# Window attention with a gated feed-forward: all local scores on the two row halves of the tensor engine, in bursts of four banks

## The chip, the cores and the metric

The kernel runs on one core of one Trainium2 chip. The metric is the device time of one execution in microseconds (us); the median of several is quoted. The engines are PE (TensorE), DVE (VectorE), ACT (ScalarE), POOL (GpSimd) and SP (SyncE, which here only issues transfers). DVE, ACT, POOL and SP are read here as working through their own instructions in the order of the program; e1, e3 and e9 each move an instruction in such an order, and what stands behind it moves too.

## The reference, cut to what matters

Eight batches of 576 positions, 8 heads of 64. A position attends to those within 32 of it; eight global positions attend to all and are seen by all. The attention's output, 4608 rows of 512, goes through a gated feed-forward and is added to it.

```python
scores = scale * np.matmul(q, k.transpose(0, 1, 3, 2))
mask = np.abs(pos[:, None] - pos[None, :]) <= window          # window = 32
mask = mask | is_global[:, None] | is_global[None, :]
attn = softmax(np.where(mask, scores, -1e9))                   # cut
x = np.matmul(attn, v)                                         # -> (4608, 512)
# ---- feed-forward, d_ff = 1536 ----
ffn_out = gelu(x @ w_gate) * (x @ w_val) @ w_out
out = x + sigmoid(x @ w_res) * ffn_out
```

## The kernel before

Rows are cut into nine chunks of 512, which is eight windows of 64. While PE does the output projection of chunk c, it also does the attention of chunk c+1 between those matmuls. Scores of a pair of heads are one full-row matmul: queries lie doubled in `qz`, with zeros in the other head's half, so that the 64 rows of the other head add nothing. Half of every streamed column is therefore zeros.

```python
def scores(c, quad, p):                       # four windows, one pair of heads: one bank
    sc = pss.tile([128, 4, 2, 64], F32, name="sc", tag="sc")      # pss: two banks
    for n in range(4):
        b, i = divmod(CH * c + 4 * quad + n, NW)
        nc.tensor.matmul(sc[:, n, :, :], kt[b % 2][:, p, 64 * i:64 * i + 128],
                         qz[b % 2][:, p, :, 64 * i:64 * i + 64], start=True, stop=True)
    ...
    nc.scalar.activation(mine, sc, ACTF.Exp, bias=0.0, scale=SCALE)      # ACT
    nc.vector.tensor_tensor(mine, mine, view(maskw, ...), ALU.mult)      # DVE

def values(c, t):                             # two windows; psn has ONE bank pair, "nd"
    nd = psn.tile([128, 2, 512], F32, name="nd", tag="nd")
    ...                                       # 4 matmuls for the globals, 16 for the windows
    nc.vector.reciprocal(r2, num[:, :, :, D])                            # DVE
    nc.vector.tensor_tensor(xtok[c % 2][:, t, :]..., num[..., 0:D], ..., ALU.mult)   # DVE, frees nd

# steady chunk: 16 jobs, each followed by a third of an output projection or a residual gate
for n in range(8):
    jobs[n].append(lambda n=n: scores(c + 1, n // 4, n % 4))
for t in range(4):
    jobs[5 + 2 * t].append(lambda t=t: values(c + 1, t))
    jobs[7 + 2 * t].insert(0, lambda t=t: turn_x(c + 1, t))
```

The first chunk has nothing to hide behind. Queries and keys of batch 0 come raw through the fast queues, are cast to bf16 (POOL, ACT, DVE), transposed by PE, copied out by ACT and DVE; then come scores, exps, values. The weights are loaded in float32 and cast meanwhile. The queries and keys of batch 2 and later, and the rows of the global positions, are loaded by transfers that POOL issues; `turn_qk` transposes them by transfers on the SP queue.

The softmax here doesn't subtract the row's maximum and nothing guards it: scores larger than these inputs give would overflow.

## Time and profile before

The median of the kernel before was 417.36 us in its first three runs and 417.56 with a fourth. I cut the span at the first gate matmul of each chunk. "Chunk 0 to 1" is chunk 0's feed-forward together with chunk 1's attention, which the program orders by hand; from then on a loop repeats.

| stage of the profiled run | us |
|---|---|
| start to first gate matmul | 30.50 |
| chunk 0 to 1 | 53.65 |
| chunk 1 | 42.59 |
| chunks 2 to 6, alternating | 42.20 / 41.97 |
| chunk 7 | 39.38 |
| chunk 8 and the end | 39.83 |

The busy table by stretches, for the kernel before; the columns are length, then busy us (and instructions) of PE, weight loads, DVE, ACT and POOL, then granted PE clock, DMA share, GB/s:

```profile
0.00:30.50 30.50, 19.38 (x244) 13.08 (x245) 18.81 (x59) 18.25 (x32) 25.17 (x47) 1.00 1.00 276
30.50:84.15 53.65, 47.64 (x353) 26.49 (x360) 33.87 (x71) 26.85 (x48) 34.24 (x39) 0.97 1.03 222
126.74:168.94 42.20, 41.94 (x304) 22.86 (x308) 22.60 (x42) 17.55 (x28) 17.18 (x19) 1.00 1.11 118
```

The third line has no room for anything but less PE work or a new PE wait. The first two have PE idle for 11 and 6 us, and in the first 30 us it is a chain of landings, casts, copies and exps that sets the end, not PE.

### The profile page before, as it was taken

What the parts mean: (1) busy time and instruction counts of PE and PEld (TensorE: products, weight loads), DVE (VectorE), ACT (ScalarE), POOL (GpSimd) and SP (SyncE); (2) the same over time, 40 slices, a digit from 0 to 9 for tenths busy, and PEclk for the clock granted to TensorE, in tenths of its full rate; (3) what the DMA queues carried; (4) which work ended last, traced back from release to release, by engine and by line L of the source; (5) the groups of instructions that cost most, each with busy time, mean ns of one, the idle gap of its engine ahead of it and who ended that gap; (6) DMA issues with size and microseconds to landing.
All of it is one profiled execution on the core that took longest, in us unless ns stands there. A gap on an engine that the chain in (4) does not pass through costs nothing.

```text
span 416.5 us, 7467 instructions
## 1 busy us (share of the span) xinstructions
PE 392.1 (94%) x2834; PEld 212.2 (51%) x2880; DVE 219.3 (53%) x437; ACT 176.0 (42%) x289; POOL 172.0 (41%) x205
## 2 busy tenths in 40 slices
PE   3788978999999999999999999999999999999995
PEld 2463555544654466446644664466446644554442
DVE  7557756635663565357635653475346543463321
ACT  5573782133623362336243624353435333623320
POOL 7987785369415531563166316441600220021012
PEclk9999989999999999999999999999999999999998
DMA  8999999149938993799279926992691210041001
GB/s 241 244 351 315 244 276 208 53 117 122 172 86 110 145 132 90 101 169 120 77 110 167 122 80 100 151 147 76 98 142 48 77 63 2 0 91 52 0 25 76
DMA packets 154900, 52.07 MB, mean 125 GB/s; under 512 B 136368, under 2 KB 147120, under 8 KB 154864
## 3 DMA queue, kind: packets, MB, share of 16 engines
q0 software_dynamic: 84768, 11.02, 43.6%
q1 hardware_dynamic: 69376, 39.52, 40.1%
q10 hardware_dynamic: 720, 1.06, 0.9%
q8 instruction: 22, 0.36, 0.4%
q14 instruction: 14, 0.11, 0.1%
HBM read 39.19 MB, written 9.44 MB: 117 GB/s over the span
## 4 chain that ended last, share of the span: by engine, by line
PE 52%; issue 27%; DMA 10%; POOL 6%; ACT 3%; DVE 1%; POOLq 0%; ACTq 0%; SPq 0%; DVEq 0%
PE v_ps L529 13%; PE g_ps L525 13%; PE f_ps L552 12%; PE r_ps L542 4%; POOL ob L558 4%; DMA wo_t<-in_k_dram 4%; PE sc L467 2%; PE nd L493 2%; DMA kt<-k_st 2%; DMA extra<-in_moe_w_out_dram 2%; DMA ht<-in_q_dram 2%; PE sn L440 1%; PE sg L418 1%; PE nd L487 1%; DMA qgf<-in_q_dram,idx 1%
## 5 line engine op out<-in xcount | busy, mean ns | idle before, releaser
L558 POOL TENSOR_TENSOR ob<-prb,xtok 128x512 f32<-128x512 f32 x36 | 41.7, 1160 | 199.2 <-DVE prb L556 196.9
L533 DVE SCALAR_TENSOR_TENSOR ht<-gsb,v_ps 128x512 bf16<-128x512 bf16 x108 | 73.5, 686 | 88.5 <-PE v_ps L529 81.1
L532 ACT ACTIVATE gsb<-g_ps 128x512 bf16<-128x512 f32 x108 | 64.4, 597 | 118.1 <-PE g_ps L525 107.5
L529 PE MATMUL v_ps<-xt,wv_t 128*128 128x512 bf16 x431 | 110.8, 379 | 1.0 <-DVE ht L533 0.5
L525 PE MATMUL g_ps<-xt,wg_t 128*128 128x512 bf16 x415 | 108.7, 379 | 1.9 <-DVE ht L533 0.7
L552 PE MATMUL f_ps<-wo_t,ht 128*128 128x512 bf16 x412 | 102.1, 379 | 3.1 <-DVE wo_t L137 2.1
L529 PEld LDWEIGHTS <-wv_t 128*128 128x128 bf16 x432 | 42.3, 98 | 51.8 <-issue 1.1
L525 PEld LDWEIGHTS <-wg_t 128*128 128x128 bf16 x432 | 42.1, 98 | 51.2 <-issue 1.8
L552 PEld LDWEIGHTS <-ht 128*128 128x128 bf16 x432 | 38.8, 98 | 37.9 <-issue 3.2
L545 ACT ACTIVATE rsb<-r_ps 128x512 bf16<-128x512 f32 x36 | 21.5, 596 | 71.8 <-PE r_ps L542 58.3
L470 ACT ACTIVATE pt<-sc 128x512 bf16<-128x512 f32 x64 | 37.4, 598 | 23.4 <-PE sc L467 23.3
L472 DVE TENSOR_TENSOR pt<-pt,maskw 128x512 bf16<-128x512 bf16 x64 | 27.2, 426 | 27.6 <-ACT pt L470 26.3
L556 DVE SCALAR_TENSOR_TENSOR prb<-rsb,f_ps 128x512 f32<-128x512 bf16 x36 | 24.6, 685 | 30.6 <-PE f_ps L552 30.4
L542 PE MATMUL r_ps<-wr_t,xt 128*128 128x512 bf16 x136 | 37.1, 385 | 0.6 <-issue 0.2
L92 POOL DMA_DIRECT2D q_st<-in_q_dram x30 | 25.8, 884 | 23.1 <-DMA qt<-q_st 23.1
L92 POOL DMA_DIRECT2D k_st<-in_k_dram x30 | 26.4, 903 | 4.1 <-DMA kt<-k_st 3.2
L467 PE MATMUL sc<-qz,kt 128*128 128x128 bf16 x256 | 24.9, 222 | 1.5 <-ACT pt L470 1.5
L467 PEld LDWEIGHTS <-kt 128*128 128x128 bf16 x256 | 19.3, 99 | 13.3 <-issue 2.5
L100 POOL DMA_DIRECT2D ve<-in_v_dram x30 | 25.5, 867 | 0.0
L507 DVE TENSOR_TENSOR xtok<-nd,rden 128x512 bf16<-128x512 f32 x34 | 23.5, 691 | 1.3
L493 PEld LDWEIGHTS <-pt 128*128 128x128 bf16 x576 | 22.2, 97 | 1.0
L493 PE MATMUL nd<-ve,pt 128*128 128x65 bf16 x320 | 22.3, 193 | 0.0
(142 smaller groups left out, 329.1 us busy)
## 6 DMA issues: line engine op xcount, KB each, us to landing
out_dram<-ob SPq DMA_DIRECT2D x36, 256.0 KB, 2.1
vo<-ve SPq DMA_DIRECT2D x12, 260.0 KB, 6.9
q_st<-in_q_dram POOLq DMA_DIRECT2D x24, 128.0 KB, 5.6
k_st<-in_k_dram POOLq DMA_DIRECT2D x24, 128.0 KB, 6.7
ve<-in_v_dram POOLq DMA_DIRECT2D x18, 128.0 KB, 6.8
wo_t<-in_k_dram SPq DMA_DIRECT2D x8, 256.0 KB, 6.9
extra<-in_moe_w_out_dram SPq DMA_DIRECT2D x4, 512.0 KB, 6.2
ve<-in_v_dram POOLq DMA_DIRECT2D x12, 96.0 KB, 6.0
```

The costliest lines, as they stand in the source:

```text
L92: nc.gpsimd.dma_start(dst[0:n, r, :].rearrange("p (h d) -> p h d", d=D), src[b].rearrange("h s d -> s h d")[128 * r:128 * r + n])
L467: nc.tensor.matmul(sc[:, n, :, :], kt[b % 2][:, p, 64 * i:64 * i + 128], qz[b % 2][:, p, :, 64 * i:64 * i + 64], start=True, stop=True)
L470: nc.scalar.activation(mine, sc, ACTF.Exp, bias=0.0, scale=SCALE)
L472: nc.vector.tensor_tensor(mine, mine, view(maskw, 0, 128, 64 * i0, [[64, 4], [0, 2], [1, 64]]), ALU.mult)
L493: nc.tensor.matmul(nds[h // 4][:, VG * (h % 4):VG * (h % 4) + VG], view(pt, 0, 128, c0, [[1, 128]]), vw, start=False, stop=(h % 4 == 3 and ...
L525: nc.tensor.matmul(g_ps, wg_t[:, kk, 128 * j:128 * j + 128], x[:, kk, :], start=(kk == 0), stop=(kk == NKT - 1))
L529: nc.tensor.matmul(v_ps, wv_t[:, kk, 128 * j:128 * j + 128], x[:, kk, :], start=(kk == 0), stop=(kk == NKT - 1))
L532: nc.scalar.activation(gsb, g_ps, ACTF.Gelu, bias=0.0, scale=1.0)
L533: nc.vector.scalar_tensor_tensor(ht[:, j, :], gsb, 0.5, v_ps, ALU.mult, ALU.mult)
L542: nc.tensor.matmul(r_ps, xt[c % 2][:, kk, 128 * t:128 * t + 128], wr_t[:, kk, :], start=(kk == 0), stop=(kk == NKT - 1))
L552: nc.tensor.matmul(held["f"], ht[:, j, 128 * t:128 * t + 128], wo_t[:, j, :], start=(j == 0), stop=(j == NFF - 1))
L558: nc.gpsimd.tensor_tensor(ob, prb, xtok[c % 2][:, t, :], ALU.add)
```

## The change

Its intent: each head's 64 rows of queries and keys use one row half of PE, two heads run side by side, and nothing is multiplied by zero. That needs one bank per half and pair of heads, so half a chunk is done at once in four banks, and its four exps and four masks follow in a burst. The doubled queries go. Weight pieces become 512 columns wide (2-KB rows), and the start and the passage from chunk 0 to 1 are reordered.

```diff
-    def scores(c, quad, p):
-        sc = pss.tile([128, 4, 2, 64], F32, name="sc", tag="sc")
-        for n in range(4):
-            b, i = divmod(CH * c + 4 * quad + n, NW)
-            nc.tensor.matmul(sc[:, n, :, :], kt[b % 2][:, p, 64 * i:64 * i + 128],
-                             qz[b % 2][:, p, :, 64 * i:64 * i + 64], start=True, stop=True)
+    def heads(c, quad, pp, sc, first):
+        for m in range(2):
+            for n in range(4):
+                b, i = divmod(CH * c + 4 * quad + n, NW)
+                for u in range(2):
+                    nc.tensor.matmul(sc[u][:, m, n, :],
+                                     kt[b % 2][64 * u:64 * u + 64, 2 * pp + m, 64 * i:64 * i + 128],
+                                     qt[b % 2][64 * u:64 * u + 64, 2 * pp + m, 64 * i:64 * i + 64], ...)
+    def scores(c, quad):
+        for pp, pool, tag in ((0, pss, "sc"), (1, psm, "mm")):
+            sc = [pool.tile([128, 2, 4, 64], F32, name="sc", tag=tag) for _ in range(2)]
+            heads(c, quad, pp, sc, True)
+            banks += [(pp, u, sc[u]) for u in range(2)]
+        for pp, u, sc in banks:
+            mine = weigh(quad, pp, u, sc)                                  # exp, ACT
+            nc.vector.tensor_tensor(mine, mine, view(maskw, ...), ALU.mult)  # mask, DVE
 ...                                                  # steady chunk
-            for n in range(8):
-                jobs[n].append(lambda n=n: scores(c + 1, n // 4, n % 4))
+            for quad in range(2):
+                jobs[1 + 4 * quad].append(lambda quad=quad: scores(c + 1, quad))
 ...                                                  # weights: 256 columns -> 512 columns, half as deep
+            for m in range(2):
+                pieces.append((src...[:, 2 * m:2 * m + 2, 512 * i:512 * i + 512], ...))
 ...                                                  # start-up
-    gather("k", 0)                                   # q, v: further down, between casts
+    for what in "kqv":
+        gather(what, 0)
-    for p in (1, 2, 3, -1):
-        for what in "kq":
-            cast_pair(0, p, what, POOL)
+    for p, by in ((0, (DVE, ACT)), (1, (DVE, ACT)), (2, (POOL, POOL)), (3, (POOL, POOL)), (-1, (POOL, ACT))):
+        for what, copy in zip("kq", by):
+            cast_pair(0, p, what, copy)              # (-1, "q") on ACT: the query remainder
     sg, ss = global_scores(0)
+    first_scores(0, 1)
+    global_exp(0, sg, ss)
     nc.vector.tensor_tensor(diag, blk[:, 0:8], blk[:, 8:16], ALU.add)
-    global_exp(0, sg, ss)                            # stood after spread_v, spread_vg
     spread_v(0, 1)
     spread_vg(0, nc.vector)
 ...                                                  # chunk 0 to 1
-            for i, n in enumerate((1, 2, 5, 6, 3, 7, 8, 9, 10, 11, 12, 13, 14, 15)):
-                if i in (1, 3, 5, 7):
-                    values(1, i // 2)
+            for i, n in enumerate((1, 5, 2, 6, 3, 7, 9, 10, 11, 13, 14, 15)):
+                if i < 4:
+                    values(1, i)
                 if i == 3:
                     load_qk(2)
                     for what in "kqv":
                         gather(what, 1)
```

Cut: the removal of `qz` with its clears and copies, the slots of the weight pieces, the place of small fills, and the weight casts of the passage, which move from DVE to POOL.

## The prediction

> **What bounds the kernel now.** I read the page's busy times first, then the busy table by stretches of time, then the timeline of one chunk and of the start-up.
>
> ```profile
> PE 392.1 (94%) x2834; PEld 212.2 (51%) x2880; DVE 219.3 (53%) x437; ACT 176.0 (42%) x289; POOL 172.0 (41%) x205
> PE   3788978999999999999999999999999999999995
> 30.40:56.00 25.60, 23.92 (x137) 11.98 (x140) 17.99 (x38) 16.23 (x31) 18.44 (x24) 1.00 1.04 286
> 56.00:66.00 10.00, 7.80 (x75) 5.44 (x76) 5.43 (x14) 8.22 (x16) 9.39 (x12) 0.83 1.79 235
> 127.80:170.00 42.20, 41.94 (x304) 22.86 (x308) 22.60 (x42) 17.55 (x28) 17.18 (x19) 1.00 1.11 118
> ```
>
> Columns of the stretches: length, then busy us of PE, weight loads, DVE, ACT, POOL, then granted clock. There are nine chunks. From chunk 1 on each takes 42.2 us and PE is busy for 41.9 of them, so only PE work, or a new PE wait, can move it. Before that there is slack: 30.5 us before the first gate matmul, then 53.8 us (30.5 to 84.3) for chunk 0's feed-forward and chunk 1's attention, 11.6 more than a steady chunk, with the clock at 0.83 in one stretch.
>
> **What the Trainium skill says.** "TensorEngine Tiling (Array Packing)", Key Properties: "Mode switching requires drain". "TensorE: Matmul & The Clock Gate", Part 3: tiles with different row groups overlap, starts about 4 ns apart; under Architectural detail, ACT and DVE are strict FIFO. "DMA: Bandwidth & Descriptors", Why small descriptors are slow: a fixed cost per packet. The trace agrees on all four. The kernel already has 64 row-half matmuls, in chunk 0 (L457). Raw starts inside a pair lie 4 ns apart and pairs 29 ns apart. The drain is seen here, in columns of start, length and what ran:
>
> ```profile
> 23.46 0.59 PE L452 MATMUL sc<-xt,ident_big 128*128 128x512 bf16 x2
> 23.99 0.41 PE L457 MATMUL sc<-qt,kt 64*128 64x64 bf16 x16
> 24.42 0.39 PE L487 MATMUL nd<-vgs,gt 128*128 128x260 bf16 x2
> ...
> 151.12 0.39 PE L467 MATMUL sc<-qz,kt 128*128 128x128 bf16 x4
> 151.34 1.03 PE L552 MATMUL f_ps<-wo_t,ht 128*128 128x512 bf16 x4
> ```
>
> Two 512-column matmuls from 23.46 stream for 2 x 0.216 (a group of four starts every 0.86), to 23.89; L457 starts at 23.99, so switching in costs 0.10. Its last start is 0.41 - 0.19 = 0.22 later, its pair is through at 24.23, and L487 starts at 24.42: switching out costs 0.19. A block of 16 is 0.53. By contrast four full-row score matmuls push the next matmul back by 0.22 (151.12 to 151.34), without a gap.
>
> **The change, part by part.** (1) Score matmuls. Removed per chunk: 8 groups x 0.22 = 1.76 us. Added: two blocks of 32, each 0.10 + 16 x 0.029 + 0.19 = 0.76, together 1.52. Gain 0.24 per chunk. Halving the streamed columns is worth 0.8; the four mode switches eat 0.6 of it.
>
> (2) The doubled queries. Twelve DVE copies (870 ns) and eight ACT copies (582 ns) go, 15 us of two engines that are about half idle. In a steady chunk PE never waited for them: worth 0. In chunk 0 the clearing of the doubled tile made PE wait for DVE three times between 38 and 42, some 1.3 us, and that goes.
>
> (3) Half a chunk in four banks. Exps and masks now come in bursts of four, and this is where I expect a loss. The second burst is issued just before the value products of the first two windows. In DVE's order, which the built program shows, all four masks stand before the reciprocal and product that empty the value bank. That bank is single and the next value products need it. Before, two masks stood on each side:
>
> ```profile
> 154.63 1.03 PE L542 MATMUL r_ps<-wr_t,xt 128*128 128x512 bf16 x4
> 155.70 0.60 ACT L545 ACTIVATE rsb<-r_ps 128x512 bf16<-128x512 f32 x1 [0.27 <-PE r_ps L542]
> 155.72 0.39 PE L487 MATMUL nd<-vgs,gt 128*128 128x260 bf16 x2
> 156.81 0.43 DVE L472 TENSOR_TENSOR pt<-pt,maskw 128x512 bf16<-128x512 bf16 x1 [0.93 <-ACT pt L470]
> 157.16 0.20 DVE L506 RECIPROCAL rden<-nd 128x8 f32<-128x8 f32 x1
> 157.39 0.69 DVE L507 TENSOR_TENSOR xtok<-nd,rden 128x512 bf16<-128x512 f32 x1
> 158.60 0.61 PE L487 MATMUL nd<-vgs,gt 128*128 128x260 bf16 x4
> ```
>
> The bank was free at 158.08 and wanted at 158.60. After the change, with S the end of the second gate's streaming (155.49 above): the tanh starts at S+0.21, exps follow every 0.49 from S+0.70, the fourth ends at S+2.77, its mask (0.42) at S+3.2, reciprocal and product end at S+4.1, PE can go on at S+4.15. PE arrives at S + 0.76 (scores) + 0.71 (values, two at 0.11 and 16 at 0.030) + 1.73 (eight down-projection matmuls) = S+3.2. So PE waits 0.95 us in each of seven chunks. Net (1)+(3): 0.95 - 0.24 = +0.7, times seven, **+5.0 us**.
>
> (4) Start-up. The three gathers are issued at once and POOL is unloaded of casts. But ACT, in order, now casts the query remainder before its first transposed copy. The last 1-KB packet of queries lands at 11.1, so that copy moves from here to about 11.8:
>
> ```profile
> 7.17 0.59 ACT L397 COPY qt<-tq 128x512 bf16<-128x512 bf16 x1 [0.37 <-PE tq L388]
> 9.67 0.59 ACT L397 COPY qt<-tq 128x512 bf16<-128x512 bf16 x1 [1.92 <-PE tq L388]
> ```
>
> From 11.2 ACT is nearly full to the first gate matmul: casts and copies 2.3, exps 1.1, copies and spread 2.2, to 17.5; global scores to 19.5; four exp pairs, two exps for the globals, two 1.05 copies, to 27; values and last transpose to about 30. Gain **0.5 us**, though q no longer waits for its gather (landed 15.0). 2-KB rows: 1-KB packets take 50 ns, 2-KB ones some 90, about 7% more rate. But four pieces, not two, are now needed before the first gate; they land by 24.5, before 30. Worth 0.
>
> (5) Chunk 0 to 1. Feed-forward in: 24 x 0.864 + 10 transposes pairs x 0.22 = 23.0 (was 24.7). Output weights are cast earlier on POOL, so waits like the last line here go:
>
> ```profile
> 56.67 1.28 ACT L470 ACT_TABLE_LOAD   x1
> 58.61 0.38 PE L467 MATMUL sc<-qz,kt 128*128 128x128 bf16 x4 [0.81 <-ACT pt L470]
> 73.87 1.45 PE L552 MATMUL f_ps<-wo_t,ht 128*128 128x512 bf16 x6 [0.74 <-DVE wo_t L137]
> ```
>
> Then globals 2.3, gate 0.9, and a wait: the scores' second bank is freed by the global exp, which stands behind tanh 0.6 and the table load 1.28, about 2.5 us. Scores, three gates, row sums and exp waits 5.5; outputs 12 x 0.864 = 10.4, values and transposes 4.0, three waits for the value bank 1.0, half clock 0.8 (it fell to half once before, and a 2.5-us hole may do it again). Sum 50.4 against 53.8: gain **3.4 us**.
>
> **Sum.** -0.5 - 3.4 + 5.0 = +1.1 on 417.4. Waits carried by hand tend to be counted in full where some overlap, so I set 417.0.
>
> **Rivals.** A: the value bank does not wait, since DVE or ACT gets through the burst sooner. The single masks' 0.93-us waits speak against it, ACT's pace being 0.49. Then seven chunks give 1.7 and the whole is about 410.5. B: row halves switch for free inside a dense stream, so 0.6 more per chunk is saved; with A that is 406. The two measured switches speak against it. C: the start-up improves by 3 us because PE warms earlier and v and gathers come sooner: 414. D: late landings or the four-bank demand on the feed-forward's banks add a second wait of 0.5 to 1 us per chunk: 423.
>
> **Range and chances.** The bank wait is good to 0.4 us x 7 = 3, the two early parts to 2 each; together about 4 to 5, and 410.5 to 423 should hold it 8 times in 10. Over 2% faster means below 409.0, which needs A together with B or C: 0.13. Over 2% slower (above 425.7) needs D and no gain in front: 0.03. Within 2%: 0.84.
>
> **What would show it.** Steady chunks of about 42.9 us; before the second value group of each chunk about 0.95 us of PE idle released by the DVE product; first gate matmul near 30; chunk 1's gate near 80; score blocks of 32 taking 0.76 with the switches. If steady chunks come out at 42.0 or less, step (3) is wrong; if the first gate starts before 28, step (4) is.

## The result, and the profile after

The changed kernel took a median of 423.75 us (422.62 to 424.90, four runs) against 417.56 us (four runs) for the kernel before. The ratio is 1.0152, 95% interval 1.0119 to 1.0185: slower, by less than 2%. Ratios here are the mean time of one kernel's fast runs over that of the other's in the same rounds, so they are not quite the ratio of the medians that I quote. The time lies 0.75 us above the stated range.

| stage | before | after | difference | predicted |
|---|---|---|---|---|
| start to first gate matmul | 30.50 | 33.09 | +2.59 | -0.5 |
| chunk 0 to 1 | 53.65 | 51.44 | -2.21 | -3.4 |
| chunk 1 | 42.59 | 43.80 | +1.21 | +0.7 |
| chunks 2 to 6 | 210.53 | 213.68 | +3.15 | +3.5 |
| chunk 7 | 39.38 | 40.36 | +0.98 | +0.7 |
| chunk 8 and the end | 39.83 | 39.84 | 0 | 0 |
| sum | | | +5.7 | +1.1 |

The page of the kernel after, its busy line and the PE row of its forty slices:

```profile
PE 390.1 (92%) x3136; PEld 203.4 (48%) x3136; DVE 204.7 (48%) x414; ACT 168.9 (40%) x279; POOL 172.6 (41%) x208
...
PE   3569978999999999999999999999999999989995
```

DVE and ACT lost 15 and 7 us of work and PE 2, and yet the span is 5.7 us longer: what was removed did not set the end. The slices show where PE thins out: the second to fourth are 5, 6, 9 where they were 7, 8, 8. The stretches, with the columns explained above:

```profile
0.00:33.09 33.09, 17.57 (x244) 12.53 (x245) 18.57 (x58) 18.76 (x32) 25.81 (x47) 1.00 0.99 298
33.09:84.53 51.44, 47.16 (x392) 25.14 (x392) 27.05 (x61) 22.40 (x38) 35.92 (x43) 0.97 0.97 199
84.53:128.34 43.81, 42.27 (x346) 21.97 (x345) 22.80 (x45) 16.81 (x28) 23.04 (x25) 1.00 1.03 123
128.34:171.11 42.77, 41.93 (x342) 21.83 (x340) 21.12 (x40) 17.13 (x28) 17.17 (x19) 1.00 1.03 116
```

A steady chunk (last line) has 42.77 us and PE busy for 41.93: 0.84 us of idle. The 0.26 of the same line of the kernel before is no wait: it is five gaps of 0.05 us at which five matmul records are missing from the trace. The timeline of that chunk shows it; columns are start, length, engine, line, operation, and in brackets the idle time before it and what ended that:

```profile
156.75 0.64 PE L449 MATMUL sc<-qt,kt 64*128 64x64 bf16 x32
157.34 2.06 ACT L456 ACTIVATE pt<-sc 128x512 bf16<-128x512 f32 x4
157.97 1.90 DVE L469 TENSOR_TENSOR pt<-pt,maskw 128x512 bf16<-128x512 bf16 x4 [1.29 <-ACT pt L456]
158.03 1.89 PE L549 MATMUL f_ps<-wo_t,ht 128*128 128x512 bf16 x8
...
160.01 0.69 DVE L504 TENSOR_TENSOR xtok<-nd,rden 128x512 bf16<-128x512 f32 x1
...
160.76 0.62 PE L484 MATMUL nd<-vgs,gt 128*128 128x260 bf16 x4 [0.84 <-DVE xtok L504]
```

The queue on DVE: four masks, one behind each exp, until 159.87, then the product that empties the value bank, until 160.70. PE wanted that bank at 159.92. The same wait, 0.84 or 0.96, stands in every chunk up to chunk 6, and 1.24 in chunk 7.

The timeline of the start, the kernel after, ACT, DVE and PE:

```profile
12.40 0.62 ACT L250 CAST q_st<-ht 128x512 bf16<-128x512 f32 x1 [4.09 <-DMA ht<-in_q_dram]
12.93 0.58 ACT L391 COPY qt<-tq 128x512 bf16<-128x512 bf16 x1
...
23.21 1.27 DVE L420 TENSOR_TENSOR gt<-gt,maskg 64x576 bf16<-64x576 bf16 x1 [2.38 <-ACT gt L418]
24.41 0.98 DVE L594 TENSOR_TENSOR diag<-blk 128x8 bf16<-128x8 bf16 x1
...
26.25 0.70 DVE L429 TENSOR_TENSOR vgs<-sn,diag 64x520 bf16<-64x520 f32 x1
...
27.00 0.39 PE L484 MATMUL nd<-vgs,gt 128*128 128x260 bf16 x2 [1.71 <-DVE vgs L429]
```

ACT sits idle for 4.09 us in front of the cast of the query remainder; the first transposed copy, which was at 7.17, is at 12.93. Later DVE does the mask of the global exps, the diagonal and the spreads one after another before the first value group, at 27.00, can begin. That was at 24.42.

### The profile page after: what moved, and what is told of

It reads as the page before. It is cut to its first block, busy times and chain, and to the rows that moved or that the text cites. A ratio compares the mean times of both kernels' runs of the same rounds, so it can differ in the third digit from the quotient of the medians.

```text
span 422.2 us, 7993 instructions
## 1 busy us (share of the span) xinstructions
PE 390.1 (92%) x3136; PEld 203.4 (48%) x3136; DVE 204.7 (48%) x414; ACT 168.9 (40%) x279; POOL 172.6 (41%) x208
## 4 chain that ended last, share of the span: by engine, by line
PE 48%; issue 28%; DMA 9%; POOL 8%; ACT 3%; DVE 2%; SPq 2%; POOLq 0%; ACTq 0%; DVEq 0%
PE v_ps L526 12%; PE g_ps L522 12%; PE f_ps L549 11%; PE r_ps L539 4%; POOL ob L555 4%; DMA extra<-in_moe_w_val_dram 3%; PE nd L490 2%; DMA extra<-in_moe_w_res_dram 2%; ACT pt L456 2%; DMA vraw<-in_moe_w_out_dram 2%; SPq L177 1%; PE sn L426 1%; PE nd L484 1%; DMA vraw<-in_v_dram 1%; DVE xtok L504 1%
## 5 line engine op out<-in xcount | busy, mean ns | idle before, releaser
L522 PE MATMUL g_ps<-xt,wg_t 128*128 128x512 bf16 x432 | 110.9, 379 | 0.7 <-ACT xt L515 0.7
L91 POOL DMA_DIRECT2D k_st<-in_k_dram x30 | 25.5, 881 | 2.8 <-DMA kt<-k_st 1.6
L484 PE MATMUL nd<-vgs,gt 128*128 128x260 bf16 x80 | 15.0, 277 | 10.0 <-DVE xtok L504 8.3
L503 DVE RECIPROCAL rden<-nd 128x8 f32<-128x8 f32 x34 | 7.0, 207 | 29.9 <-PE nd L490 28.4
```

The costliest lines, as they stand in the source:

```text
L91: nc.gpsimd.dma_start(dst[0:n, r, :].rearrange("p (h d) -> p h d", d=D), src[b].rearrange("h s d -> s h d")[128 * r:128 * r + n])
L522: nc.tensor.matmul(g_ps, wg_t[:, kk, 128 * j:128 * j + 128], x[:, kk, :], start=(kk == 0), stop=(kk == NKT - 1))
```

## The experiments

All kernels of this section gave correct results. Edits are shown against the kernel after unless said otherwise. Ten ran; "first gate" is the start of the first gate matmul.

| run | median us | ratio to before (95%) | first gate | chunk 0 to 1 | chunk 1 | steady |
|---|---|---|---|---|---|---|
| before | 417.6 to 418.0 | 1 | 30.50 | 53.65 | 42.59 | 42.20/41.97 |
| after | 423.75 | 1.0152 (1.0119, 1.0185) | 33.09 | 51.44 | 43.80 | 42.77/42.68 |
| e1_values_first | 415.75 | 0.9958 (0.9934, 0.9982) | 35.28 | 49.28 | 41.94 | 41.77/41.55 |
| e2_diag_first | 423.14 | 1.0137 (1.0107, 1.0166) | 34.33 | 49.28 | 43.07 | 42.77/42.68 |
| e4_old_start | 419.64 | 1.0051 (1.0024, 1.0078) | 30.10 | 50.18 | 43.39 | 42.77/42.68 |
| e6_half_by_half | 424.60, one run | none | 34.43 | 50.27 | 43.48 | 42.94/42.84 |
| e3_diag_qlate | 423.17 | 1.0112 (1.0063, 1.0160) | 29.07 | 49.32 | 49.28 | 42.78/42.67 |
| e5_rows_1k | 424.26 | 1.0146 (1.0098, 1.0194) | 33.66 | 49.28 | 43.54 | 42.77/42.68 |
| e7_all | 411.94 | 0.9857 (0.9789, 0.9924) | 29.03 | 51.24 | 43.37 | 41.77/41.55 |
| e8_old_start_fixed | 411.11 | 0.9838 (0.9785, 0.9891) | 29.36 | 49.98 | 42.86 | 41.77/41.55 |
| e9_gathers_later | 408.46 | 0.9773 (0.9757, 0.9789) | 30.02 | 46.84 | 44.05 | 41.77/41.55 |
| e10_qlate_gathers | 416.99 | 0.9980 (0.9964, 0.9997) | 29.55 | 50.15 | 43.06 | 42.77/42.68 |

The first two stages carry noise. PE's clock is first granted in full at a different time in each run (18.20 in after, 25.20 in e1, which has the same start), and a stretch of half clock of 3.41 us falls into one of these stages, or into neither (in e7 it lies across the end of the second; in e3 one of twice that length falls into chunk 1). Chunk lengths from chunk 2 on repeat to 0.02 us.

For the passage from chunk 0 to 1 the record shows what decides. Within each run all changes of the granted clock lie whole multiples of 3.413 us apart: they stand on a grid of windows, and where that grid lies against the program differs from run to run. The passage has one PE wait of 2.29 us. In after, e4 and e10 it lies inside one window, and the next window runs at half clock (e6 the same, with 2.08 us). In e1, e2, e3 and e5 the edge of a window cuts the same wait in two, and the clock stays. Busy table of the window of the wait in after, then of the two windows that share it in e1:

```profile
59.16:62.57 3.41, 1.12 (x35) 0.81 (x34) 0.45 (x1) 3.35 (x5) 2.81 (x4) 1.00 0.78 213
59.33:62.75 3.42, 2.04 (x29) 1.18 (x28) 0.18 (x1) 1.47 (x2) 2.82 (x3) 1.00 0.57 200
62.75:66.16 3.41, 2.36 (x67) 1.42 (x66) 1.55 (x4) 3.35 (x7) 3.12 (x5) 1.00 0.65 145
```

How little PE work a window may hold is not settled: the clock fell after a window with PE busy for 1.97 us in the kernel before (55.60 to 59.02), and stayed after one with 1.38 in e8 (77.31 to 80.72).

### e1: the masks of the second burst behind the first value product

```diff
-        for pp, u, sc in banks:
-            mine = weigh(quad, pp, u, sc)
-            nc.vector.tensor_tensor(mine, mine, view(maskw, ...), ALU.mult)
+        mines = [weigh(quad, pp, u, sc) for pp, u, sc in banks]
+        def masks():
+            for mine in mines:
+                nc.vector.tensor_tensor(mine, mine, view(maskw, ...), ALU.mult)
+        return masks
 ...
+            def second():                 # job 5
+                masks = scores(c + 1, 1)
+                values(c + 1, 0)          # these windows belong to the first burst
+                masks()
```

> The changed kernel with one thing moved: the four masks of a chunk's second score burst are issued on DVE after the reciprocal and product that empty the value bank, not before. Bank theory (the steady loss is PE waiting about 1.0 us per chunk for the single value bank, whose emptying stands behind four masks): the idle before the second value group goes from 1.0 to under 0.1 us, steady chunks from 42.7 to 41.7 us, the whole from 423.75 to about 417, start and first chunk unchanged. Switch theory (the loss is the drain at each change between row halves and full rows): nothing moves, 423 to 424. Burst theory (four banks at once hold up the feed-forward's banks): chunks stay near 42.7 with the wait appearing elsewhere.

The timeline of the same place in a steady chunk of this run:

```profile
155.51 2.06 ACT L456 ACTIVATE pt<-sc 128x512 bf16<-128x512 f32 x4
...
156.20 1.89 PE L553 MATMUL f_ps<-wo_t,ht 128*128 128x512 bf16 x8
...
156.65 0.69 DVE L508 TENSOR_TENSOR xtok<-nd,rden 128x512 bf16<-128x512 f32 x1
157.25 1.42 DVE L471 TENSOR_TENSOR pt<-pt,maskw 128x512 bf16<-128x512 bf16 x4
...
157.93 0.61 PE L488 MATMUL nd<-vgs,gt 128*128 128x260 bf16 x4
```

The product now comes first, the bank is free at 157.34, and PE goes on at 157.93 without a wait. Steady chunks fall from 42.77/42.68 to 41.77/41.55, and chunk 7 from 40.36 to 38.95; that is about 0.17 more each than the idle time that the trace lists. The whole falls by 8.0 us, though the first gate came 2.2 us later here than in the profile of after. The bank wait is shown to be the cost in the steady chunks, and the change of the score matmuls alone is worth 42.20 - 41.77 = 0.43 us a chunk.

### e2: the diagonal and the spreads ahead of the global exps

```diff
+    nc.vector.tensor_tensor(diag, blk[:, 0:8], blk[:, 8:16], ALU.add)
+    spread_v(0, 1)
+    spread_vg(0, nc.vector)
     global_exp(0, sg, ss)
-    nc.vector.tensor_tensor(diag, blk[:, 0:8], blk[:, 8:16], ALU.add)
 ...
-    spread_v(0, 1)
-    spread_vg(0, nc.vector)
```

> The changed kernel with the diagonal, the gathered values' cast and their spread put before the global exponentials, as the kernel before had them. Theory of DVE order (in the start-up these three, 1.9 us, stand between the mask of the globals and the row sums, and the first value group waits for the last of them): first value group from 27.0 to about 25.3, first gate matmul from 33.1 to about 31.4, the whole 1.7 us less. Rival (the start is bound by ACT, which waits for the last query transfer until 12.4): DVE's order is worth less than 0.5, first gate stays near 32.7.

The DVE wait in front of the first value group is gone. But the query remainder was cast at 13.74 in this run (12.40 in the profile of after), and the first value group began at 28.24, which is 14.50 behind that cast; in the kernel after it was 14.60. In e1, which has the same start as after and ran on the same chip, the cast was at 13.67 and the first value group at 29.20. So the repair gave at most 1 us, of which part may be the clock: it was first granted in full at 23.62 here and at 25.20 in e1. The DVE queue was real, but ACT's queue was right beside it.

### e4: the start-up of before, everything else changed

The edit puts back the block from the first cast to the last `first_scores`, word for word, and the single gather in front.

> The changed kernel with the whole start-up order of the kernel before (gathers, casts, masks, globals), all else changed. If the loss in the start-up comes from the reordering alone: first gate matmul back at 30.5 (33.1 changed), the whole 421 to 421.5. If the new weight pieces (four needed for the first gate) or the absent doubled queries have a share: first gate later than 31 or earlier than 30.

The busy table of this run by stretches:

```profile
0.00:30.10 30.10, 19.16 (x244) 12.94 (x245) 17.48 (x57) 17.69 (x30) 25.57 (x48) 0.89 1.00 288
30.10:80.28 50.18, 47.16 (x392) 25.17 (x392) 28.67 (x61) 22.38 (x38) 37.37 (x44) 0.97 1.07 224
```

The first gate is back at 30.10, and the whole is 4.1 us faster than after (423.75 to 419.64, against the same kernel before, whose medians differ by 0.2). That is what the reordering of the start-up costs. What stays, 1.9 us over before, is the loss of chunks 1 to 7 less the gain of the passage.

### e6: one row half after the other

```diff
-        for m in range(2):
-            for n in range(4):
-                for u in range(2):
+        for u in range(2):
+            for m in range(2):
+                for n in range(4):
```

> The changed kernel with the score matmuls of a block issued eight heads of one row half and then eight of the other, not in turn. If the gain of the new scores comes from two halves running side by side, a block of 32 grows from 0.57 us to about 1.0 (32 x 0.027 plus the switch) and each chunk by up to 0.9 us in two blocks, though part may hide in the wait for the value bank. If the array overlaps successive matmuls of one half as well, the block stays near 0.6.

The timeline of a block of 32 score matmuls and the next matmul, first in the kernel after, then here:

```profile
150.54 1.02 PE L539 MATMUL r_ps<-wr_t,xt 128*128 128x512 bf16 x4
151.50 0.64 PE L449 MATMUL sc<-qt,kt 64*128 64x64 bf16 x32
152.07 2.76 PE L549 MATMUL f_ps<-wo_t,ht 128*128 128x512 bf16 x12
```

```profile
150.39 1.02 PE L539 MATMUL r_ps<-wr_t,xt 128*128 128x512 bf16 x4
151.35 0.81 PE L449 MATMUL sc<-qt,kt 64*128 64x64 bf16 x32
152.09 2.76 PE L549 MATMUL f_ps<-wo_t,ht 128*128 128x512 bf16 x12
```

From block to next matmul it is 0.57 with the halves alternating and 0.74 in the new order: alternating is worth 0.17 a block, 0.34 a chunk. That is neither of the two results expected, and it is not the worth of running side by side, because the new order did not stop it. In the single records of this block all 32 starts lie within 0.62 us, one every 20 ns, while the first five, all of one half, are about 29 ns apart: from the sixth on, starts of the second half fall between those of the first. Without any overlap the same stretch would take about 1.05 us (32 x 0.029 and the 0.12 to the next matmul; an estimate). So side by side is worth more than 0.17 a block, perhaps up to 0.5, and no run here separates it. A steady chunk grew by only 0.17, because the bank wait shrank from 0.84 to 0.67: what PE does longer, it waits less. This was one run, so its total is not used.

### e3: as e2, and the query remainder cast after the first scores

```diff
-    for p, by in (..., (-1, (POOL, ACT))):
+    for p, by in (..., (-1, (POOL, None))):
 ...
     first_scores(0, 0)
+    cast_pair(0, -1, "q", ACT)
```

> As e2_diag_first, and the cast of the query remainder is issued on ACT after the first score exponentials, not ahead of the first transposed copy. ACT theory (in the start-up ACT stands still 4 to 5 us for the last query transfer, and everything behind it is late and runs at half clock): first transposed copy near 9, first scores near 10 as in the kernel before, first gate matmul 30 to 31, the whole about 419 (e2: 423.14). Gather theory (the early gathers hold up the other transfers, so the late landing is felt wherever the cast stands): first gate stays above 33, the whole 422 to 423.

The start did what it should. ACT's timeline here:

```profile
8.18 0.58 ACT L391 COPY qt<-tq 128x512 bf16<-128x512 bf16 x1
...
12.85 0.62 ACT L250 CAST q_st<-ht 128x512 bf16<-128x512 f32 x1 [1.25 <-DMA ht<-in_q_dram]
```

The first transposed copy is at 8.18 instead of 14.27 in e2, the first gate at 29.07 instead of 34.33 (33.09 in after); e7 and e10, with the same start, have 29.03 and 29.55. So one cast in the wrong place cost 5.3 us of start-up against e2, from which e3 differs by nothing else, and 4.0 (e2's repair included) against the profile of after. But the whole did not move: 423.17. Chunk 1 took 49.28 us. Its PE and SP timeline:

```profile
91.21 6.58 SPq L398 DMA_TRANSPOSE kt<-k_st  x5
...
101.31 0.26 PE L409 MATMUL ss<-qgz,kt 128*128 128x16 bf16 x4 [0.48 <-DMA kt<-k_st]
103.02 0.26 PE L409 MATMUL ss<-qgz,kt 128*128 128x16 bf16 x4 [1.45 <-DMA kt<-k_st]
104.22 0.28 PE L409 MATMUL ss<-qgz,kt 128*128 128x16 bf16 x4 [0.94 <-DMA kt<-k_st]
```

The stretch of half clock in it, in the busy table (the last three columns are clock, DMA share and GB/s):

```profile
103.58:110.41 6.83, 6.19 (x48) 2.58 (x49) 2.15 (x5) 3.57 (x7) 1.49 (x2) 0.50 2.04 190
```

PE came earlier, and met the transposed keys of batch 2, which did not: three waits, 2.9 us together, and from 103.58, between the second and the third, 6.83 us at half clock, which costs up to half of that. Those keys come at the end of a queue. POOL issues the loads and gathers, then does the sums `ob` of chunk 0's output; SP stores these and behind the stores issues the ten transposes. The kernel after has the same queue, but reaches this place at 107.4 and does not feel it.

### e5: weight pieces of 256 columns as before

The edit puts back the loop over 256-column pieces.

> The changed kernel with the weight pieces of the kernel before (256 columns, 1-KB rows), all else changed. My reading: weights land before they are needed either way, so the first gate and the whole stay within 1 us of the changed kernel (423.75), while packets go from 88 to about 50 ns and the landing of the twelfth piece moves back by 1 to 2 us. Rival: the 2-KB rows carry part of the faster first chunk, which would then grow by 1 us or more.

It took 424.26 us, ratio 1.0146, where after has 1.0152. The 2-KB rows are worth nothing in time that these runs can show, though the packets moved faster (mean of the packet records of the first 33 us: 91 ns for 2 KB in after, 52 ns for 1 KB here): the weights were not what the first gate waited for.

### e7 and e8: the repairs together

e7 is e1 and e3, and in the passage from chunk 0 to 1 the global exps go ahead of the residual gate and the value groups are spaced as before. e8 is the same with the whole old start in place of e3's.

```diff
             held = global_scores(1)
-            work_f[0]()
             global_exp(1, *held)
+            work_f[0]()
 ...
-                if i < 4:
-                    values(1, i)
-                if 1 < i < 6:
-                    turn_x(1, i - 2)
+                if i in (1, 3, 5, 7):
+                    values(1, i // 2)
+                if i in (3, 5, 7, 9):
+                    turn_x(1, i // 2 - 1)
```

> e1 and e3 together, and in chunk 0 the global exponentials ahead of the first gate and the value groups two work items apart as before. If the parts add: steady chunks 41.7, first gate 30 to 31, chunk 0 to 1 about 47.5 (the 2.3-us wait for the global exponential shorter by 1.5, 1.6 us of waits for the value bank gone), together 408 to 410, faster than both kernels. If the early parts only trade one wait for another: 412 to 415.

> The same as e7_all, but with the whole start-up order of the kernel before in place of the mended new one. First gate 30.1 to 30.5, chunk 0 to 1 about 47.5, steady 41.7, together about 408.5. If it is faster than e7_all, the reordered start-up has nothing to keep; if slower by 1 or more, the early gathers and the shared casts are worth something once ACT no longer waits.

Both beat before, though not surely by 2%: 411.94 and 411.11 us. Chunk 2 began at 123.64 and 122.21, against 128.34 in after. Of the passage's waits the one of 2.29 us for the global exp is gone (two for the exps of the scores, 0.78 together, stand in its place), and those for the value bank went too. But a new one stood in front of chunk 1's first gate, 4.46 us in e7 and 3.22 in e8. The timeline of e8 there:

```profile
76.10 0.95 POOL L285 DMA_INDIRECT vgf<-in_v_dram,idx  x1 [0.30 <-issue]
77.07 2.27 POOL L558 TENSOR_TENSOR ob<-prb,xtok 128x512 f32<-128x512 f32 x2
...
78.27 0.69 DVE L556 SCALAR_TENSOR_TENSOR prb<-rsb,f_ps 128x512 f32<-128x512 bf16 x1 [4.74 <-POOL ob L558]
...
79.34 1.02 PE L525 MATMUL g_ps<-xt,wg_t 128*128 128x512 bf16 x4 [3.22 <-DVE xt L518]
```

PE waits for DVE's copy of the transposed rows; DVE, in order, stands before that copy at a product whose buffer POOL has to empty; and POOL is still issuing three gathers that nobody needs before chunk 1 is half done.

### e9 and e10: the gathers at the beginning of chunk 1

e9 is e8, and e10 is e3, each with this edit:

```diff
                 if i == 3:
                     load_qk(2)
-                    for what in "kqv":
-                        gather(what, 1)
 ...                                       # beginning of chunk 1
-                for n in range(2, B // 2):
+                for n in range(1, B // 2):
                     for what in "kqv":
                         gather(what, n)
```

> This is the run with the old start and the mended middle, with one thing more: batch 1's three gathers are issued by GpSimd together with the others at the beginning of chunk 1, not in front of the first output sums. In that run the tensor engine stood 3.22 us in front of chunk 1's first gate matmul: the DVE product of the outputs had waited 4.74 us for GpSimd's output sums, and GpSimd was issuing gathers (73.4 to 77.1) while they waited. Theory (GpSimd's order): the sums run 3.9 us earlier, the 3.22 us shrink to under 0.7, chunk 1 begins near 76.5 and its transposed loads, which the SyncE queue issues behind those outputs, are earlier too, so that the 0.8 us wait for them in chunk 1 goes as well; steady chunks stay at 41.77/41.55; the whole 407.5 us (406 to 409.5). Rival (the gain is given back): the later gathers push the v and k loads of the next batches back, chunk 1 grows by the 3 us gained, and the whole stays at 411 +- 0.8.

> This is the run with the query remainder cast late and the global rows spread early (first gate 29.07, but chunk 1 49.28 us long, whole 423.2), with batch 1's gathers issued at the beginning of chunk 1. Theory (the GpSimd queue holds the output sums, the sums hold the output stores in SyncE's queue, the stores hold the transposed k loads of batch 2): the transposes are issued some 4 us earlier, the three waits of the tensor engine for kt in chunk 1 (2.9 us together) go, no half clock follows them, chunk 1 takes 43.1 and chunk 2 begins near 121.5; the whole 417.0 us (415.5 to 418.5). Rival 1 (the k loads themselves land late, whatever the order behind them): the waits stay, chunk 1 takes 48 to 49.5, the whole 422 to 424. Rival 2 (the half clock comes by itself after a long dense stretch, not from the waits): waits gone, half clock stays, chunk 1 some 46, the whole 420.

The timeline of e9:

```profile
74.48 2.39 POOL L558 TENSOR_TENSOR ob<-prb,xtok 128x512 f32<-128x512 f32 x2
...
76.87 1.02 PE L525 MATMUL g_ps<-xt,wg_t 128*128 128x512 bf16 x4
...
101.46 0.26 PE L408 MATMUL ss<-qgz,kt 128*128 128x16 bf16 x4 [1.96 <-DMA kt<-k_st]
```

The sums begin 2.6 us earlier, the gap of 3.22 us is gone, and chunk 1 begins at 76.87 instead of 79.34. The whole is 408.46 us, 2.3% under before: the best version. One part of what I expected failed. The wait for the keys in chunk 1 did not go but grew from 0.77 to 1.96: PE came 2.5 us earlier, and the transposes only 1.5 (issued from 88.90 instead of 90.41). In this profiled run, the slowest of the four, 1.2 of the 2.5 us were so given back at the next place in the same queue.

e10 took 416.99 us, 6.2 less than e3. The waits for the keys and the half clock in chunk 1 are gone, and chunk 1 takes 43.06. The total is as expected, but not quite by my route. The key transposes were issued 1.5 us earlier (89.66 to 91.21), not 4, and PE came 1.3 us later, because a half clock fell into the passage. Both together were enough. The theory of the queue is supported by the direction of both runs; the claim that the edit alone would move the keys by 4 us failed.

## Why the prediction was wrong

The result is within 2%, as was thought most likely, but outside the range. Taken by its own steps:

**Step (3), the value bank: right.** It predicted 0.95 us of PE idle in each chunk, released by the DVE product. Measured were 0.84 and 0.96, and 1.24 in chunk 7, at the place named and from the releaser named (1.00 to 1.41 by what e1 takes off a chunk); e1 takes the wait away by order alone and nothing else takes its place. Rival A is out, and so is rival D for the steady chunks: with that wait gone, e1 has no PE wait from its first gate of chunk 1 to the end of chunk 7.

**Step (1), the score matmuls: right in kind, too small.** It counted 0.76 for a block with its two switches. The residual gate streams until 151.40 (four times 0.216 from 150.54), and the next matmul after the block starts at 152.07: 0.67. The gain is 8 x 0.22 - 2 x 0.67 = 0.42 a chunk, not 0.24, and e1 measures 0.43 against before. I had taken the switch out of the half mode from a place where value products follow (0.19). Rival B, switches for free, is out all the same: 32 matmuls in 16 pairs 29 ns apart are 0.46, and 0.67 was paid. Steps (1) and (3) together gave +0.6 to +0.7 a chunk, where +0.7 was said.

**Step (2), the doubled queries: right.** DVE and ACT lost the work, and no steady chunk gained by it. The waits of PE for DVE between 38 and 42 (1.23 us in the kernel before) went, as said.

**Step (4), the start-up: this is the step that failed.** It said that the first gate comes 0.5 us earlier; it came 2.6 later (3.2 to 4.8 in e5, e6 and e1, which have the same order at the start), and e4 puts the price at 4.1 us of the whole: with the old order the kernel takes 419.64 us, inside the stated range. The chain was the right one: ACT, in order, stood at the query remainder. The term that failed is the last, "to 27; values and last transpose to about 30". The first value group did begin at 27.00. But from the first value group to the first gate it is 6.09 us, not 3: 24.42 to 30.50 in the kernel before, 27.00 to 33.09 in the kernel after, and 6.08 to 6.09 in every experiment. I had that row in hand and did not read it. With it the same chain gives 33.1, which is what happened.

That the chain came to 27 was luck. The copy that I put at about 11.8 began at 12.93, because the remainder was usable at 12.40, not at 11.2; and the second score exps began at 21.24, not 19.5. Against these 1.7 us, the sum counts one pair of score exps too many: chunk 0 has four in all, and I had one in "exps 1.1" and four more behind. From there ACT needed 5.8 us, not 7.5. The sum was also only made for ACT. DVE had its own queue of five instructions up to 26.95, which is what released the first value group in this run; e2 shows that it cost little only because ACT's was as long. Rival C is out: PE's clock was first granted in full 3.3 us earlier than before (18.20 against 21.47), and the start was still later.

The worth of 2-KB rows, "about 7% more rate", does not follow from the 50 and 90 ns given with it (11%); it was booked as 0, and e5 shows no difference.

**Step (5), the passage: right in kind, and too large by 1.2 in the profile of after.** The wait for the global exp was predicted at 2.5 us and measured at 2.29. The half clock was counted at 0.8, and that was right: the stage takes 49.28 without it (e1, e2, e5) and 50.18 and 50.15 with it (e4, e10), which is a gain of 3.5 on the kernel before, which has one too, where 3.4 was said. The kernel after has 1.3 us more, and with them two waits for the value bank of 1.07 and 0.35 us; every other run with this passage has a single one above 0.2 there, of 0.22 or 0.23. In front of the longer wait DVE took up the reciprocal 0.95 us after the last value matmul (0.04 in e4), and the trace does not show why. So the three waits of 1.0 in the forecast are not what the passage usually does.

**The sum.** Against +1.1 predicted there are +5.7: 3.1 from step (4), 1.2 from step (5) and 0.35 from chunks 1 to 7. Those of step (5) contain the two waits just named, and those of the chunks a single PE stall of 0.58 at 96.5; no other run showed either at that place, and I cannot explain them. Without the stall the chunks would be 0.2 under the prediction. I then rounded the sum down, "waits carried by hand tend to be counted in full"; here they were counted short.

**What the prediction did not see at all** is that the early stages are tied to a transfer. A kernel that is 4 us faster at the first gate is not 4 us faster at the end if a queue through POOL, SP and the transposes decides when chunk 1 may go on. e3 shows it at its plainest: 4 us gained on the kernel after at the first gate, 0.6 at the end. In the changed kernel itself this was hidden by its slow start.

**Open.** How much PE work a window needs for the clock to stay; why the kernel after alone had the stalls at 72.9 and 96.5; what bounds the keys of batch 2 in e9, where 1.96 us remain; how much of e10's gain is the edit and how much the place of the half clock. e4's 4.1 us are measured, but its split between the cast and the DVE order is only bounded (e2, e3), since moving one moves the other's wait.

## What to carry to other kernels

When work is gathered into bursts, look in each engine's order for the short instruction that frees a buffer and now stands behind the burst; moving four masks behind one product was worth 8 us here, more than the 6.2 us by which the whole change had made the kernel slower. On an engine that runs in order, an instruction that waits for a late landing must stand behind everything that is ready. And before you book a gain in an early stage, follow the next transfer's chain of issue through every queue in front of it: an engine that gets there earlier waits there longer.

## What the Trainium skill lacked or had wrong

- "TensorEngine Tiling (Array Packing)", Key Properties, says that switching the mode drains the engine, without a size. In the blocks of 32 score matmuls both switches together cost 0.67 - 0.46 = 0.21 us, about 0.10 each; in front of value products, in the kernel before, the switch back took 0.19.
- "TensorE: Matmul & The Clock Gate", Part 1, has the clock fall to half after an idle window of about 3.4 us, with windows that run free of the kernel. Length and grid agree: 3.413 us, and whole multiples of it between all changes of a run. But the window before a fall was not idle: PE was busy for 1.97 us of it in the kernel before, with no single wait over 0.81, and for 1.12 in the kernel after. How much work keeps the clock up, no page says.
- "DMA: Bandwidth & Descriptors", Anatomy of one DMA, calls the generation of descriptors small, which it is not for a kernel that issues many transfers from POOL; another row of the page, under Latency and other measured facts, puts the emission on this path at about 1 us, and that fits. On POOL five loads took 4.3 us of the engine in every run (0.86 each) and a gather, around chunk 1, 0.94 to 1.08 us with 0.30 between two. Ten loads and three gathers stood 12 us in front of POOL's sums, and in e8 that reached PE as a gap of 3.22 us.
